# A gated pair of cached attentions on one core: the rows of the query weights dealt to the partitions in another order

## The chip, the cores and the metric

The kernel runs on one core of a Trainium2 chip. A core has a matrix engine (TensorE, PE in the profile), a vector engine (VectorE, DVE), a scalar engine (ScalarE, ACT), GpSimd (POOL) and SyncE (SP), which here does nothing but issue transfers. Sixteen DMA engines bring data from the chip's memory into the on-chip memory of 128 partitions. The metric is the device time of one execution in microseconds (us), as the median over several runs.

## The reference

There are two blocks, A and B, each a decode step of attention with its own weights and its own cache; one vector x per batch (2 batches, 512 numbers) goes into both, and a gate mixes the results.

```python
def block(x, k_cache, v_cache, wq, wo):          # x 2x1x512, caches 2x32x4096x128
    q = (x @ wq).reshape(2, 1, 32, 128).transpose(0, 2, 1, 3)
    scores = einsum("bhqd,bhkd->bhqk", q, k_cache) * 128 ** -0.5
    o = einsum("bhqk,bhkd->bhqd", softmax(scores), v_cache)
    return o.transpose(0, 2, 1, 3).reshape(2, 1, 4096) @ wo

g = sigmoid((x * gate_w).sum(-1, keepdims=True))
out = g * A(x) + (1 - g) * B(x)
```

All numbers are f32. Each wq is 512 x 4096 and each wo 4096 x 512, 8 MB apiece; each of the four caches is 128 MB.

## The kernel before

**Tiles and units.** All large data come in tiles of 128 partitions x 16384 numbers, 64 KB to a partition and 8 MB in all. There are three such buffers on chip: two called kt (for K, and at first for wq) and one called vt (for V). The work is cut into 32 units (2 blocks x 2 batches x 8 groups of four heads). For each unit one tile of K and one of V are loaded. VectorE multiplies K by the query in place (L257) and sums over the 128 numbers of a head (L262), which gives the scores; it takes their maximum (L264 to L268). ScalarE takes exponentials (L304, L307) and scales some slots of V (L313); TensorE multiplies them with V (L371), GpSimd handles the last slots of V (L336, L345). At the end both results are multiplied with wo (L424, L442) and written out.

**The order of the loads.** SP issues every large load, into one queue, in an order written out by hand (L122 to L235): wq of A and of B into the two kt buffers (L123); the first tile of K in two halves (L215, L216), once TensorE has finished A's projection; the second K tile and the first V tile (L212, L219), once B's projection is finished; then by turns the next K (L212), once VectorE has summed the K tile that lay there, and the next V (L228), once TensorE has finished with V. ScalarE's queue loads x (2 rows of 512) and the gate's row (L124, L125).

**The start, which the change touches.** wq has 512 rows. Partition p holds its rows 4p to 4p + 3, which are 64 KB in one piece ("block p" below). The projection contracts over the partition and over c, the row in the block, so x has to stand with its number 4p + c on partition p. The three rows (x of both batches and the gate's row) lie on three partitions of a buffer (`raw`, in qr0). TensorE turns them with four transposes, one for each c, which read every fourth number (L174); VectorE copies the result out of PSUM (`xg`, L158), scales x into `xs` (L160), multiplies x with the gate's row (L161) and sums (L163). A matmul with ones adds up over the partitions (L180), and VectorE makes g and 1 - g of it. The projection (L190) waits for wq and for `xs`; ScalarE brings its result to on-chip memory (L195), and further matmuls spread each query to the partitions of its head (L201).

**Semaphores** that the text names: x (x and the gate's row have landed), h (GpSimd's constants), e (VectorE's steps at the start and the end), y (TensorE's), k0 and k1 (the loads into the two kt buffers).

Of the kernel before, what the change touches and what calls it, by code (L numbers as in the profile page):

```python
# [13 lines left out]
B = 2  # L14
# [4 lines left out]
KC = D // P  # L19
# [17 lines left out]
UB = B * HG  # L37
CUT = UB - 2
PAD = 96
SCALE = DH ** -0.5  # L40
ACT3 = 3
DVE5 = 5
# [4 lines left out]
def tile_gated_decode(ctx: ExitStack, tc: tile.TileContext, ins: dict, out: bass.AP):  # L47
    nc = tc.nc
    lead = ctx.enter_context(tc.tile_pool(name="lead", bufs=1))
    lead.tile([P, PAD], F32, name="pad")  # L50
    big = ctx.enter_context(tc.tile_pool(name="big", bufs=1))
# [5 lines left out]
    def sb(name, shape):  # L57
        return small.tile(shape, F32, name=name)
# [4 lines left out]
    ident, ones = sb("ident", [P, P]), sb("ones", [P, P])  # L63
# [7 lines left out]
    vs, qr = sb("vs", [P, VC * DH]), [sb(f"qr{i}", [P, HG // 2, DH]) for i in range(2)]  # L71
    rl, ot, on = sb("rl", [P, HU]), sb("ot", [P, 2, B * H]), [sb(f"on{n}", [P, NJ, B]) for n in "AB"]
    xg, xw, zp, gate = sb("xg", [P, B + 1, KC]), sb("xw", [P, B, KC]), sb("zp", [P, B]), sb("gate", [P, 4, B])
    raw, xs = qr[0].rearrange("p g d -> p (g d)")[:B + 1], vs[:, :KC * QP].rearrange("p (c q) -> p c q", c=KC)
    rows, bs = qr[1][:H, :B], qr[0].rearrange("p g d -> p (g d)")
    res = qr[1].rearrange("p g d -> p (g d)")[:B]
# [5 lines left out]
    def sem(name):  # L82
        return tc.alloc_semaphore(name)

    sk, s_kb, s_v, s_x, s_out = [sem("k0"), sem("k1")], sem("kb"), sem("v"), sem("x"), sem("out")
    s_t = [sem(f"t{i}") for i in range(len(TAIL) + 2)]
    s_d, s_n, s_e = sem("d"), sem("n"), sem("e")
    s_a, s_c, s_p, s_o, s_y, s_g, s_h = (sem(x) for x in ("a", "c", "p", "o", "y", "g", "h"))
    ctx.enter_context(tc.tile_critical(sync_engine=mybir.EngineType.Pool))

    def wait(engine, *pairs):
        for s, v in pairs:
            engine.wait_ge(s, v)  # L93
# [3 lines left out]
    def inc(s, i):  # L97
        i.then_inc(s, 1)
        count[id(s)] = count.get(id(s), 0) + 1
        return count[id(s)]  # L100
# [16 lines left out]
    pe, dve, act, pool, sp = nc.tensor, nc.vector, nc.scalar, nc.gpsimd, nc.sync  # L117


    half = BIG // 2  # L120
    wq = {n: ins[n + "_wq"].rearrange("(p c) f -> p (c f)", c=KC) for n in "AB"}
    for i, n in enumerate("AB"):  # L122
        sp.dma_start(kbuf[i], wq[n]).then_inc(sk[i], 16)  # L123
    act.dma_start(raw[:B], ins["A_x"].rearrange("b s e -> (b s) e")).then_inc(s_x, 16)  # L124
# [14 lines left out]
    def e(i):  # L139
        return inc(s_e, i)  # L140
# [7 lines left out]
    for b in range(B):  # L148
# [5 lines left out]
    wait(dve, (s_h, READY), (s_e, head_at))  # L154
    const_at = e(dve.tensor_copy(heads.rearrange("p (a h) -> p a h", h=HP)[:, :, :HU],
                                 head[:, None, :].to_broadcast([P, VC, HU])))
    wait(dve, (s_y, 1))
    xg_at = e(dve.tensor_copy(xg, mix[:, 0, :KC * (B + 1)].rearrange("p (c r) -> p r c", c=KC)))  # L158
    wait(dve, (s_e, xg_at))
    xs_at = e(dve.tensor_scalar(xs[:, :, :B].rearrange("p c b -> p b c"), xg[:, :B], SCALE, None, op0=ALU.mult))  # L160
    xw_at = e(dve.tensor_tensor(xw, xg[:, :B], xg[:, B:].to_broadcast([P, B, KC]), op=ALU.mult))  # L161
# [7 lines left out]
    e(dve.tensor_scalar(gate[:, 3], gate[:, 2], -1.0, 1.0, op0=ALU.mult, op1=ALU.add))  # L169


    wait(pe, (s_x, 32), (s_h, 2))
    for c in range(KC):
        i = pe.transpose(mix[:, 0, c * (B + 1):(c + 1) * (B + 1)],  # L174
                         raw.rearrange("r (p c) -> r c p", c=KC)[:, c], ident[:B + 1, :B + 1])
        if c < 2:
            i.then_inc((s_p, s_o)[c], 1)
    i.then_inc(s_y, 1)
# [300 lines left out]
```

## Time and profile before

| what | before |
|---|---|
| median of 3 runs | 1324.2 us (1324.03 to 1324.35) |
| the profiled execution's own time | 1324.36 us |
| its span, first to last instruction | 1322.5 us |
| VectorE busy | 1136.7 us (86%) |
| TensorE busy | 446.2 us (34%) |
| GpSimd busy | 378.4 us (29%) |
| ScalarE busy | 174.2 us (13%) |
| bytes read | 570.43 MB, 431 GB/s over the span |

The profile is that of one execution. Its span lies 1.9 us under the execution's own time; the rest is outside the first and last instruction. A row of a timeline gives the start, the length in us, the engine, the line of the code, the operation and the tiles that it writes and reads; in brackets stands how long the engine sat idle before it and what ended that. A name with a q at its end (SPq, PEq) is an engine's sequencer, where issues of transfers stand. In a row of windows stand the window and its length, then for PE, the weight load of PE, DVE, ACT and POOL the busy us and the count of instructions, then the granted clock of TensorE, the mean busy share of the 16 DMA engines and the GB/s that they moved.

### The profile page before, as it was taken

The page shows a single profiled execution, that of the slowest core. Times are in us where ns is not written, and L with a number is a line of the kernel's source. Part 1 is how long each engine was busy: PE and PEld are TensorE (multiplying, and loading weights), DVE is VectorE, ACT ScalarE, POOL GpSimd, SP SyncE. Part 2 cuts the span into 40 slices and gives each one's busy share as a digit, 9 for nine tenths or more (in the row PEclk, how much of TensorE's full clock was granted, in tenths as well). Part 3 has the DMA queues.
Part 4 walks back from the last instruction along what each step waited for, and adds up shares of the span by engine and source line. Part 5 has one row for each costly group of instructions (what it writes and reads, how often), then busy time and mean ns, then how long its engine had stood idle before and what let it go on. Part 6 is the DMA issues. An engine that isn't in the chain of part 4 may idle for free.

```text
span 1322.5 us, 6956 instructions
## 1 busy us (share of the span) xinstructions
PE 446.2 (34%) x2344; PEld 176.9 (13%) x2344; DVE 1136.7 (86%) x249; ACT 174.2 (13%) x611; POOL 378.4 (29%) x202
## 2 busy tenths in 40 slices
PE   3303333223333231335323133332313333231376
PEld 1001110101111010111111011111101111110132
DVE  0399999989999999999999899999999999999960
ACT  0001110110111011011101111110111111111110
POOL 0003333212333321233332133333213333311350
PEclk9756666556666655666665566666556666655668
DMA  9999999999999999999999999999999999999998
GB/s 412 441 416 442 442 416 444 438 418 442 442 416 444 442 430 428 442 436 422 441 440 420 440 440 420 442 442 432 428 440 436 424 440 440 420 440 440 420 443 352
DMA packets 10962, 570.54 MB, mean 431 GB/s; under 512 B 1221, under 2 KB 1477, under 8 KB 1738
## 3 DMA queue, kind: packets, MB, share of 16 engines
q1 hardware_dynamic: 10948, 570.43, 99.6%
q8 instruction: 4, 0.07, 0.0%
q14 instruction: 4, 0.03, 0.0%
q10 hardware_dynamic: 6, 0.01, 0.0%
HBM read 570.43 MB, written 0.00 MB: 431 GB/s over the span
## 4 chain that ended last, share of the span: by engine, by line
DMA 51%; DVE 28%; issue 20%; PE 1%; DVEq 0%; SPq 0%; ACT 0%; POOLq 0%
DMA kt<-in_B_k_cache_dram 26%; DVE sc L262 23%; DMA kt<-in_A_k_cache_dram 21%; DVE kt L257 3%; DMA kt<-in_B_wo_dram 3%; DMA kt<-in_A_wq_dram 2%; DVE kt L274 1%; DVE sc L276 1%; PE mix L190 0%; PE q L190 0%; DVE rl L244 0%; DVEq L93 0%; PE q L442 0%; SPq L235 0%; DVEq L257 0%
## 5 line engine op out<-in xcount | busy, mean ns | idle before, releaser
L257 DVE TENSOR_TENSOR kt<-kt,q 128x16384 f32<-128x16384 f32 (+1 forms) x32 | 542.5, 16954 | 83.0 <-DMA kt<-in_B_k_cache_dram 47.6
L262 DVE TENSOR_REDUCE sc<-kt 128x128 f32<-128x16384 f32 (+1 forms) x32 | 542.5, 16953 | 1.9
L371 PE MATMUL vp<-vt,pr 128*32 128x512 f32 x1550 | 256.6, 773 | 700.5 <-DMA vt<-in_A_v_cache_dram 371.8
L336 POOL TENSOR_TENSOR vt<-vt,pp 128x2560 f32<-128x2560 f32 x31 | 138.4, 4465 | 891.6 <-DMA vt<-in_A_v_cache_dram 495.6
L345 POOL TENSOR_TENSOR vt<-vt 128x1536 f32<-128x1536 f32 (+2 forms) x93 | 219.5, 2360 | 7.4
L371 PEld LDWEIGHTS vp<-vt,pr 128*32 128x32 f32 x1550 | 82.5, 138 | 850.7 <-issue 845.1
L313 ACT ACTIVATE vt<-vt,pp 128x128 f32<-128x128 f32 x248 | 75.9, 388 | 592.7 <-DMA vt<-in_A_v_cache_dram 296.9
L371 PE MATMUL vp<-vt,heads 128*32 128x512 f32 x62 | 56.5, 1012 | 112.5 <-POOL vt L345 112.5
L304 ACT ACTIVATE pr<-sc,nm 32x100 f32<-32x100 f32 (+1 forms) x128 | 60.1, 470 | 112.4 <-DVE nm L268 110.9
L376 PE MATMUL ol<-strip,vs 128*128 128x4 f32 x256 | 58.8, 353 | 24.4 <-ACT vs L316 24.4
L316 ACT ACTIVATE vs<-vp 128x512 f32<-128x512 f32 x32 | 19.1, 597 | 360.9 <-PE vp L371 360.9
L376 PEld LDWEIGHTS ol<-strip,vs 128*128 128x128 f32 x256 | 56.1, 323 | 76.3 <-issue 74.7
L274 DVE TENSOR_TENSOR kt<-kt,q 128x8192 f32<-128x8192 f32 x1 | 8.7, 8686 | 39.9 <-DMA kt<-in_A_k_cache_dram 39.9
L304 ACT ACTIVATION_READ_ACCUMULATOR pr<-sc,nm 32x1 f32 x128 | 24.2, 189 | 0.0
L371 PEld LDWEIGHTS vp<-vt,heads 128*32 128x32 f32 x62 | 5.3, 133 | 140.6 <-POOL vt L345 140.6
L453 DVE COPY qr<-q 2x128 f32<-2x128 f32 x2 | 0.6, 282 | 22.1 <-PE q L442 22.1
L244 DVE RECIPROCAL rl<-ol 128x4 f32<-128x4 f32 x32 | 5.6, 176 | 14.7 <-PE ol L379 14.7
L379 PE MATMUL ol<-ltot,ones 128*128 128x4 f32 x64 | 18.0, 351 | 0.0
L190 PE MATMUL mix<-kt,vs 128*32 128x512 f32 x64 | 11.5, 887 | 17.4 <-DMA kt<-in_A_wq_dram 10.6
L379 PEld LDWEIGHTS ol<-ltot,ones 128*128 128x128 f32 x64 | 17.2, 329 | 0.0
L307 ACT ACTIVATE pp<-sc,nm 128x28 f32<-128x28 f32 (+1 forms) x32 | 10.2, 318 | 0.9
L264 DVE TENSOR_REDUCE rm<-sc 128x1 f32<-128x128 f32 x32 | 9.2, 286 | 1.1
(77 smaller groups left out, 139.1 us busy)
## 6 DMA issues: line engine op xcount, KB each, us to landing
kt<-in_A_k_cache_dram SPq DMA_DIRECT2D x2, 4096.0 KB, 25.7
kt<-in_B_wo_dram SPq DMA_DIRECT2D x1, 4096.0 KB, 32.5
kt<-in_B_wo_dram SPq DMA_DIRECT2D x3, 1024.0 KB, 36.6
kt<-in_B_wo_dram SPq DMA_DIRECT2D x1, 512.0 KB, 39.3
vt<-in_A_v_cache_dram SPq DMA_DIRECT2D x16, 24.7
kt<-in_B_k_cache_dram SPq DMA_DIRECT2D x16, 42.2
kt<-in_B_wo_dram SPq DMA_DIRECT2D x1, 256.0 KB, 39.5
kt<-in_B_wo_dram SPq DMA_DIRECT2D x2, 128.0 KB, 39.4
```

The costliest lines, as they stand in the source:

```text
L257: dve.tensor_tensor(k, k, q[:, None, :].to_broadcast([P, SLOTS - first, DH]), op=ALU.mult).then_inc(s_d, 1)
L262: dve.tensor_reduce(s[:, first:], k, axis=AX.X, op=ALU.add).then_inc(s_d, 1)
L274: m = e(dve.tensor_tensor(k1, k1, qall[:, None, A0:A0 + DH].to_broadcast([P, SLOTS // 2, DH]), op=ALU.mult))
L276: m = e(dve.tensor_reduce(sc[0][:, :SLOTS // 2], k1, axis=AX.X, op=ALU.add))
L304: x = act.activation(w, sc[u % 2][r, :f * VC].rearrange("p (c a) -> p c a", a=VC), AF.Exp, bias=nm[u % 2][r], accum_out=lsum[r, h:h + 1])
L313: x = act.activation(v[:, t], v[:, t], AF.Copy, scale=pp[u % 2][:, t:t + 1])
L316: act.activation(vs, vp, AF.Copy).then_inc(s_a, 1)
L336: pool.tensor_tensor(w[:, :m], w[:, :m], pp[j][:, :m, None].to_broadcast([P, m, DH]), op=ALU.mult).then_inc(s_g, 1)
L345: pool.tensor_tensor(x, x, y, op=ALU.add).then_inc(s_g, 1)
L371: x = pe.matmul(vp[s * QP:(s + 1) * QP], pr[:, c] if c < f else heads, v[:, c], start=c < STRIPS, stop=c > f - STRIPS)
L376: pe.matmul(ol[:, 0], vs[:, a * DH:(a + 1) * DH], strip[:, a * HP:a * HP + HU], start=a == 0, stop=a == VC - 1)
L379: pe.matmul(ol[:, 1], ones, ltot, start=True, stop=True).then_inc(s_o, 1)
```

## The change

Partition 8a + b (a from 0 to 15, b from 0 to 7) now takes block 16b + a of wq, for A and for B alike. In the pattern of the load, the memory's side has 16 groups (a) that lie one block of 64 KB apart, and in each group 8 blocks (b) that lie 16 blocks, 1 MB, apart. As the projection sums over all partitions, the order doesn't matter as long as x follows: a new copy on VectorE brings the three rows into that order, into `cols`, which lies in qr1, a buffer that is free then. With the copy the four numbers of a block also come apart, so that each transpose now reads 128 neighbouring numbers. VectorE's copy waits for x and the gate's row; TensorE's first transpose waits for the copy, where before it waited for x and the gate's row itself. The gate's sum over all partitions doesn't depend on the order. The loads of K, V and wo are as they were.

```diff
+LANES = 16
...
+    cols = qr[1].rearrange("p g d -> p (g d)")[:B + 1].rearrange("r (c p) -> r c p", c=KC)
...
-    wq = {n: ins[n + "_wq"].rearrange("(p c) f -> p (c f)", c=KC) for n in "AB"}
+    wq = {n: ins[n + "_wq"].rearrange("(b a c) f -> a b (c f)", c=KC, a=LANES) for n in "AB"}
     for i, n in enumerate("AB"):
         sp.dma_start(kbuf[i], wq[n]).then_inc(sk[i], 16)
...
+    wait(dve, (s_x, 32))
+    order_at = e(dve.tensor_copy(cols.rearrange("r c (a b) -> r c a b", a=LANES),
+                                 raw.rearrange("r (b a c) -> r c a b", c=KC, a=LANES)))
     wait(dve, (s_y, 1))
...
-    wait(pe, (s_x, 32), (s_h, 2))
+    wait(pe, (s_e, order_at), (s_h, 2))
     for c in range(KC):
         i = pe.transpose(mix[:, 0, c * (B + 1):(c + 1) * (B + 1)],
-                         raw.rearrange("r (p c) -> r c p", c=KC)[:, c], ident[:B + 1, :B + 1])
+                         cols[:, c], ident[:B + 1, :B + 1])
```

After the change the lines below the edits stand 2 to 5 higher in number.

## The prediction

> **What bounds the kernel now.** I read the page first: its line of DMA shares by slices, its queues, and the bytes.
>
> ```profile
> span 1322.5 us, 6956 instructions
> ...
> DMA  9999999999999999999999999999999999999998
> GB/s 412 441 416 442 442 416 444 438 418 442 442 416 444 442 430 428 442 436 422 441 440 420 440 440 420 442 442 432 428 440 436 424 440 440 420 440 440 420 443 352
> ...
> q1 hardware_dynamic: 10948, 570.43, 99.6%
> ...
> HBM read 570.43 MB, written 0.00 MB: 431 GB/s over the span
> ```
>
> Every slice of the DMA line but the last has a 9, and one queue, q1 (SP's), holds the 16 DMA engines for 99.6% of the span. So the time is the sum of what that queue moves. A tile of 128 x 16384 f32 is 8.389 MB, so q1's 570.43 MB are 68 such loads (two of wq, 64 of the caches, two of wo). Next the busy time of a long stretch in the middle, and the chain of waits in order of time (start, length, what):
>
> ```profile
> 100.00:1250.00 1150.00, 376.53 (x1868) 152.29 (x1868) 1057.86 (x210) 160.22 (x570) 357.14 (x180) 0.59 1.00 434
> ```
>
> ```profile
> 426.45 42.17 DMA kt<-in_A_k_cache_dram
> ...
> 503.73 42.16 DMA kt<-in_A_k_cache_dram
> ```
>
> In the middle the DMA share is 1.00 and the rate 434 GB/s; 8.389 MB at that rate are 19.33 us. The chain says the same: its loads of K begin 503.73 - 426.45 = 77.28 us apart, in which four loads (two K, two V) pass, so 19.32 us each. The 128 rows of a load, 64 KB each and one to a partition, fall on 16 engines, eight rows to each: 19.32 / 8 = 2.415 us a row, 27.1 GB/s an engine. That pace is even (42.17 and 42.16 in the two rows), with every engine busy. So bytes alone give 68 x 19.32 = 1313.8 us of the 1322.5, and only a change in the pace of a load, or in the gaps at the two ends, can move the end.
>
> The change touches the first two loads. Their issues (KB and the median us from issue to landing are the columns; with one load the median is its time), and when SP issued them:
>
> ```profile
> kt<-in_A_wq_dram SPq DMA_DIRECT2D x1, 22.1
> kt<-in_B_wq_dram SPq DMA_DIRECT2D x1, 41.0
> ```
>
> ```profile
> 0.89 0.40 SPq L123 DMA_DIRECT2D kt<-in_A_wq_dram  x1
> ...
> 1.35 0.42 SPq L123 DMA_DIRECT2D kt<-in_B_wq_dram  x1
> ```
>
> A's weights land at 0.89 + 22.1 = 23.0 us, which is 22.1 - 19.32 = 2.8 us more than a load at the pace of the middle: the start. B's land at 1.35 + 41.0 = 42.35, 19.36 behind A's: full pace already. Whatever the new order of addresses is good for, the most it can give back is that 2.8 and 0.04 us.
>
> **The change part by part.** Two edits: the pattern of the two wq loads, and a copy on VectorE in the way of x. First the copy. Of VectorE, the piece between its constants and the gate's sum (spread, deal and heads are constants; xg is x and the gate's row turned onto partitions; e, h, x, y are semaphores), before and then now:
>
> ```order
> L153 COPY deal<-ident 32x32 [waits e]
> L155 COPY heads<-head 128x4x4 [waits e,h]
> L158 COPY xg<-mix 128x12 [waits y]
> L160 TENSOR_SCALAR vs<-xg 128x2x4 [waits e]
> L161 TENSOR_TENSOR xw<-xg 128x8
> ```
>
> ```order
> L155 COPY deal<-ident 32x32 [waits e]
> L157 COPY heads<-head 128x4x4 [waits e,h]
> L160 COPY qr_92<-qr_91 3x512 [waits x]
> L163 COPY xg<-mix 128x12 [waits y]
> L165 TENSOR_SCALAR vs<-xg 128x2x4 [waits e]
> ```
>
> One copy of 3 x 512 has come in, and the wait on x has moved from TensorE's first transpose to it; TensorE now waits for the copy. What is queued behind that wait on VectorE is xg, which comes after the transposes anyway, and then nothing until the first product on K. The rows of the timeline that price it and that cover it:
>
> ```profile
> 2.23 0.70 DVE L149 COPY spread<-ident 128x128 f32<-128x128 f32 x2
> ...
> 10.49 0.64 PE L174 MATMUL mix<-ident,qr 3*128 3x3 f32 x4 [10.49 <-DMA qr<-in_gate_w_dram]
> 11.17 0.17 DVE L158 COPY xg<-mix 128x12 f32<-128x12 f32 x1 [8.09 <-PE mix L174]
> 11.38 0.17 DVE L160 TENSOR_SCALAR vs<-xg 128x8 f32<-128x8 f32 x1
> ...
> 23.04 5.49 PE L190 MATMUL mix<-kt,vs 128*32 128x512 f32 x32 [10.58 <-DMA kt<-in_A_wq_dram]
> ...
> 28.35 3.61 PE L190 MATMUL q<-kt,vs 128*32 128x512 f32 x32
> ...
> 32.02 0.33 SPq L215 DMA_DIRECT2D kt<-in_A_k_cache_dram  x1
> ...
> 42.39 6.05 PE L190 MATMUL mix<-kt,vs 128*32 128x512 f32 x32 [6.80 <-DMA kt<-in_B_wq_dram]
> ...
> 51.94 0.33 SPq L212 DMA_DIRECT2D kt<-in_A_k_cache_dram  x1
> ```
>
> A copy of 12 columns takes 0.17 us and one of 128 columns 0.35 (0.70 for two); 512 columns lie between 0.35 (length free) and 4 x 0.35 = 1.4. I take the line through the two rows: 0.17 + 500 x 0.18 / 116 = 0.95, and with a hand-over 1.1 us. It stands between x's landing at 10.49 and the scaled x, ready at 11.38 + 0.17 = 11.55. That is first read at 23.04, when A's weights are there: 11.5 us of cover. So the copy costs nothing; without the cover it would cost 1.1 us.
>
> Now the loads. Of SP, its first loads before and now (kt_62 and kt_63 are the two K buffers):
>
> ```order
> L123 DMA kt_62<-in_A_wq_dram 128x16384
> L123 DMA kt_63<-in_B_wq_dram 128x16384
> L215 DMA kt_62<-in_A_k_cache_dram 128x8192 [waits y]
> L216 DMA kt_62<-in_A_k_cache_dram 128x8192
> L212 DMA kt_63<-in_A_k_cache_dram 128x16384 [waits y]
> ```
>
> ```order
> L125 DMA kt_62<-in_A_wq_dram 128x1x16384
> L125 DMA kt_63<-in_B_wq_dram 128x1x16384
> L220 DMA kt_62<-in_A_k_cache_dram 128x8192 [waits y]
> L221 DMA kt_62<-in_A_k_cache_dram 128x8192
> L217 DMA kt_63<-in_A_k_cache_dram 128x16384 [waits y]
> ```
>
> No load has moved, and the bytes and the 64 KB rows are the same; the shape is not. Every big load of before has 128 rows on both sides. The two wq loads now have 128 rows on the side of the partitions and 16 groups of eight on the side of the memory. No transfer in the trace has unequal sides. My reading is that 16 groups on 16 engines are dealt one to each: engine a reads blocks a, 16 + a, 32 + a and so on, and writes partitions 8a to 8a + 7 one after the other.
>
> On the reading side that is harmless: 16 neighbouring blocks at a time. On the writing side the rows of before only say that its own dealing, whatever it is, lets each engine write 27.1 GB/s with none in another's way, since no load falls below it. A new dealing can keep that or lose it, it can't better it. If on-chip memory is entered by groups of partitions that are not eight neighbours, then engines that march in step through eight neighbours each meet in pairs at half of the entries, while the other half stand idle, and after four rows all change over together. Then every row takes two shares: 2 x 2.415 = 4.83 us, a load 38.64, and the two loads together cost 2 x 19.32 = 38.6 us more. The bounds are 0 (no two meet; then the wq rows themselves, at 19.36, are the price) and 38.6. The nearest row, the old wq load, has the old dealing, and the dealing is the one thing that is new, so I don't take its price; I take the upper end.
>
> [...]
>
> Does anything hide the 38.6? A's weights would land at 23.0 + 19.3 = 42.3, its projection takes 32.02 - 23.04 = 9.0, so the two halves of the first K go out at 51.3; B's weights hold the queue until 42.35 + 38.64 = 81.0, so it doesn't run dry. B's projection (51.94 - 42.39 = 9.55) lets SP issue the second K at 90.6, while the first K runs until 81.0 + 19.32 = 100.3: 9.7 us of cover, as before. Behind that the order and the waits of SP are unchanged, and all 66 remaining loads come 38.6 us later. Nothing has slack against a queue at 99.6%. x may land later too, behind rows of twice the length: by 21 at most (twice 10.49), and 21 + 1.1 + 1.1 = 23.2 is still ahead of 42.3.
>
> The sum: copy 0, wait 0, loads + 38.6. On the profiled execution's 1324.36 that is 1363.0, and that execution lies 0.16 over the median of 1324.2, so 1362.8.
>
> **The rivals.** *One engine of a pair goes first.* If an entry serves the first comer in full, the other waits four rows once, 4 x 2.415 = 9.7 us; from then on the two are at different entries, and the lag is carried through. That gives 1324.2 + 9.7 = 1333.9. Nothing in the trace speaks of how engines share an entry; that all rows keep one pace speaks for even sharing, hence the smaller chance.
>
> *Not slower: the dealing costs nothing.* Either the rows are dealt as before whatever the shape of the source, or an engine's 2.415 us a row is its own limit and not that of the entry, and where it writes is all one. For it: no row shows an entry as the limit. Point that decides: two engines on one entry must together move less than 2 x 27.1 GB/s. Then copy and loads come to 0, and the time is 1324.2.
>
> *Faster: the new order mends the start.* Sixteen neighbouring blocks at a time, instead of blocks far apart in the 8 MB, could be read quicker. The most is 2.84 us, 1321.4. Against it: B's load has the old order and full pace, and so have the loads of K and V, dealt alike. [...]
>
> **How the numbers follow.** Pairs in step 0.67; one first 0.13; nothing 0.17; start mended 0.03. The first gets the most because a dealing by 16 groups is what the pattern asks for, and only one arrangement of entries (eight neighbours each) would leave it unpunished. The likeliest gives 1362.8. For the range: below, the one-sided case, 1333.9, rounded out to 1333.5; above, sharing that also loses a start of 2.8 us in each load, 1362.8 + 5.6 = 1368.4, so 1368.5. Left out is 0.20. Within 0.2% (2.6 us, about what a measurement of this kernel can tell from no change): the third case and a third of the fourth, 0.18; faster by more 0.02; slower 0.80.
>
> **What would show it.** In the changed profile: wq landing at about 41 and 80 us after issue instead of 22.1 and 41.0; about half of 434 GB/s in the first two slices and the third; the first product on K (L274 before, L279 now) at 92 instead of 53; and from there the old pitch of 77.28. The copy should show as about 1 us on VectorE, with TensorE waiting for weights behind it. Landings of 22 and 41 would prove the forecast wrong, and so would a queue that runs dry between the wq loads and the first K, which would add to it.

## The result, and the profile after

The changed kernel takes 1366.46 us (median of 6 runs, 1366.30 to 1366.54) against 1324.2 before: a ratio of 1.0319 (95% interval 1.0308 to 1.0329), 42.3 us slower. The profiled execution's span is 1364.7 us, 42.2 more than before. On the page, the DMA lines by 40 slices of 34 us:

```profile
DMA  9999999999999999999999999999999999999998
GB/s 215 200 321 432 430 442 444 430 434 430 430 432 430 448 438 432 432 430 430 432 431 450 434 432 432 430 432 432 430 450 434 432 432 430 434 430 434 448 431 349
...
q1 hardware_dynamic: 10948, 570.43, 99.6%
```

The first line looks as it did: a 9 in every slice but the last, 99.6% for q1, the same packets and bytes. Only the second line tells: 215, 200 and 321 GB/s where 412, 441 and 416 stood, and from the fourth slice on the old rate. The windows put numbers to it (the last three columns are the granted clock, the busy share of the 16 DMA engines, and GB/s), the first within the two wq loads:

```profile
7.00:83.00 76.00, 14.12 (x78) 4.71 (x78) 1.69 (x9) 1.37 (x3) 0.00 (x0) 0.87 1.00 207
```

```profile
142.80:1292.80 1150.00, 375.91 (x1868) 153.72 (x1868) 1058.36 (x210) 160.19 (x570) 357.44 (x180) 0.59 1.00 434
```

Both have a share of 1.00; in the first the engines move 207 GB/s, in the second 434. So the busy share doesn't tell an engine at full pace from one at half of it. How they go through the rows can be seen in a stretch within B's load, 46 to 78 us in slices of 0.8 us, where each transfer is counted in the slice in which it begins:

```profile
GB/s 0 0 1311 0 0 0 0 0 983 328 0 0 0 0 246 1065 0 0 0 0 0 1229 82 0 0 0 0 1147 164 0 0 0 0 410 901 0 0 0 0 0
```

1311 GB/s over 0.8 us are 16 rows of 64 KB, as many as there are engines. They begin within one slice or two, and the next 16 begin about 5 us later: the engines march in step, and none runs ahead of the others. The issues of wq, and the rows of the timeline that answer to those of before:

```profile
kt<-in_A_wq_dram SPq DMA_DIRECT2D x1, 43.3
...
kt<-in_B_wq_dram SPq DMA_DIRECT2D x1, 83.1
```

```profile
0.89 0.69 SPq L125 DMA_DIRECT2D kt<-in_A_wq_dram  x1
...
1.64 0.57 SPq L125 DMA_DIRECT2D kt<-in_B_wq_dram  x1
...
13.48 0.61 DVE L160 COPY qr<-qr 3x512 f32<-3x512 f32 x1 [10.41 <-DMA qr<-in_gate_w_dram]
14.14 0.58 PE L179 MATMUL mix<-ident,qr 3*128 3x3 f32 x4 [14.14 <-DVE qr L160]
14.77 0.17 DVE L163 COPY xg<-mix 128x12 f32<-128x12 f32 x1 [0.68 <-PE mix L179]
...
44.27 5.88 PE L195 MATMUL mix<-kt,vs 128*32 128x512 f32 x32 [28.22 <-DMA kt<-in_A_wq_dram]
...
53.66 0.38 SPq L220 DMA_DIRECT2D kt<-in_A_k_cache_dram  x1
...
84.80 6.10 PE L195 MATMUL mix<-kt,vs 128*32 128x512 f32 x32 [27.58 <-DMA kt<-in_B_wq_dram]
...
94.40 0.33 SPq L217 DMA_DIRECT2D kt<-in_A_k_cache_dram  x1
...
95.72 8.69 DVE L279 TENSOR_TENSOR kt<-kt,q 128x8192 f32<-128x8192 f32 x1 [78.85 <-DMA kt<-in_A_k_cache_dram]
```

A's weights land at 44.2 instead of 23.0, B's at 1.64 + 83.1 = 84.74 instead of 42.35: 40.5 us behind A's, where a load took 19.4. That is 5.07 us for each of an engine's eight rows of 64 KB, 2.1 times 2.415. The first product on K starts 42.6 us later than before, where its row was

```profile
53.14 8.69 DVE L274 TENSOR_TENSOR kt<-kt,q 128x8192 f32<-128x8192 f32 x1 [39.88 <-DMA kt<-in_A_k_cache_dram]
```

and the rest follows at the old pitch; the chain of after has it:

```profile
468.78 42.16 DMA kt<-in_A_k_cache_dram
...
546.05 42.16 DMA kt<-in_A_k_cache_dram
```

546.05 - 468.78 = 77.27 us for four loads, as before. So the whole loss lies in the two wq loads, 21 us in each.

### The profile page after: what moved, and what is told of

Read it like the earlier page. It is cut to its first block, busy times and chain, and to the rows that moved or that the text cites. A ratio compares the mean times of both kernels' runs of the same rounds, so it can differ in the third digit from the quotient of the medians.

```text
span 1364.7 us, 6957 instructions
## 1 busy us (share of the span) xinstructions
PE 444.5 (33%) x2344; PEld 177.4 (13%) x2344; DVE 1137.3 (83%) x250; ACT 174.1 (13%) x611; POOL 378.8 (28%) x202
## 3 DMA queue, kind: packets, MB, share of 16 engines
q1 hardware_dynamic: 10948, 570.43, 99.6%
## 4 chain that ended last, share of the span: by engine, by line
DMA 52%; DVE 27%; issue 19%; PE 1%; DVEq 0%; SPq 0%; ACT 0%; POOLq 0%
DMA kt<-in_B_k_cache_dram 25%; DVE sc L267 22%; DMA kt<-in_A_k_cache_dram 22%; DVE kt L262 3%; DMA kt<-in_A_wq_dram 3%; DMA kt<-in_B_wo_dram 3%; DVE kt L279 1%; DVE sc L281 1%; PE mix L195 0%; PE q L195 0%; DVE rl L249 0%; DVEq L95 0%; PE q L447 0%; SPq L240 0%; DVEq L262 0%
## 5 line engine op out<-in xcount | busy, mean ns | idle before, releaser
L195 PE MATMUL mix<-kt,vs 128*32 128x512 f32 x64 | 12.0, 916 | 55.8 <-DMA kt<-in_A_wq_dram 28.2
L429 PE MATMUL q<-vt,onA 128*2 128x512 f32 x64 | 9.1, 728 | 4.8 <-DMA vt<-in_A_wo_dram 4.8
## 6 DMA issues: line engine op xcount, KB each, us to landing
kt<-in_B_k_cache_dram SPq DMA_DIRECT2D x16, 42.2
```

The costliest lines, as they stand in the source:

```text
L195: i = pe.matmul(r[h * QP:(h + 1) * QP], xs[:, c], cols[:, c, h, half_ * HG // 2:(half_ + 1) * HG // 2, :], start=c == 0, stop=c == KC - 1)
```

## The experiments

The trace says where the time went, not why. The theory is that of the prediction: 16 groups are dealt one to an engine, an engine then writes eight neighbouring partitions, and engines meet in pairs where they write. The dealing, and entries at which engines could meet, are assumptions of mine: no view names the engine of a row or shows an entry. Three rivals could lose the same 42 us in the same place: the path of x (copy and wait), the order of reading (neighbouring blocks at once), and the shape (a pattern of two levels is slow in itself).

**The copy alone.** The loads as before, the copy in x's own order:

```diff
-    wq = {n: ins[n + "_wq"].rearrange("(b a c) f -> a b (c f)", c=KC, a=LANES) for n in "AB"}
+    wq = {n: ins[n + "_wq"].rearrange("(p c) f -> p (c f)", c=KC) for n in "AB"}
...
-                                 raw.rearrange("r (b a c) -> r c a b", c=KC, a=LANES)))
+                                 raw.rearrange("r (a b c) -> r c a b", c=KC, a=LANES)))
```

> The copy on VectorE and its wait stay, the loads have their old pattern, and x keeps its old order. Theory (engines meet in pairs where they write): the copy is covered, 0.6 us of VectorE beside 9 us of slack before the weights land; 1324.2, within 0.5. Rival (the path of x is what costs): up to 1366.

Measured: 1324.1 us, ratio 1.0 (0.9991 to 1.0009). The copy takes 0.60 us at 10.53, and the path of x is out.

**Groups of four instead of eight.** Against the changed kernel, one number:

```diff
-LANES = 16
+LANES = 32
```

> The same change with 32 groups of four instead of 16 groups of eight: partition 4a + b takes block 32b + a, with x in that order. The pattern has two levels as in the changed kernel and neighbouring blocks are still read at the same time, but a group is four neighbouring partitions and no longer eight. Theory (meeting where they write): if 32 groups are dealt so that an engine again keeps one entry for itself, wq lands at 22.1 and 41.0 as before, and the time is 1324.2, within 1. Rival (reading): neighbouring blocks at once are slow to read; 1366, or between. Rival (shape): a pattern of two levels is slow in itself; 1366.

Measured: 1324.62 us, ratio 1.0003 (0.9994 to 1.0013). Its wq issues, and the window within the two loads:

```profile
kt<-in_A_wq_dram SPq DMA_DIRECT2D x1, 22.6
...
kt<-in_B_wq_dram SPq DMA_DIRECT2D x1, 41.2
```

```profile
7.00:39.00 32.00, 13.32 (x78) 4.54 (x78) 1.68 (x9) 1.37 (x3) 0.00 (x0) 1.00 0.98 426
```

Two levels in the pattern, neighbouring blocks read at once (16 of 32, if each engine takes its rows in order), the same copy, and the loads run at their old pace: the projections of A and B start at 23.56 and 42.86, 19.3 us apart. With that the shape is out as a cause, and so is the hope that such an order of reading mends the start: A lands 22.6 us after issue, B 41.2, against 22.1 and 41.0. Which two groups an engine gets stands in no view. Two neighbouring ones would be the eight partitions of the changed kernel again, and by the theory as slow; so the old pace fits the theory only if they are dealt otherwise. A slow run would not have refuted the theory. The next run is the stronger test: by the theory a piece of it reaches half of the entries, whichever engine writes which row.

**Halves of the partitions.** Against the kernel before, the blocks in their old order:

```diff
+    s_w = [sem("w0"), sem("w1")]
...
-        sp.dma_start(kbuf[i], wq[n]).then_inc(sk[i], 16)
+        sp.dma_start(kbuf[i][:P // 2], wq[n][:P // 2]).then_inc(s_w[i], 16)
+        sp.dma_start(kbuf[i][P // 2:], wq[n][P // 2:]).then_inc(sk[i], 16)
...
-        wait(pe, (sk[n], 16), (s_e, xs_at), (s_c, c0))
+        wait(pe, (s_w[n], 16), (sk[n], 16), (s_e, xs_at), (s_c, c0))
```

> The kernel before, with each wq load cut into two: partitions 0 to 63, then 64 to 127. Old order of the blocks, plain pattern, the same 64 KB rows, 16 engines with four rows each per piece. Theory (meeting): a piece reaches half of the entries, so two engines share one, at the 5.06 us a row of the changed kernel: (84.74 - 44.22) / 8. Each load 40.5, landing at about 42 and 83 us after issue, 1324.2 + 42.3 = 1366.5. Rivals (reading, shape): nothing has changed for them; 1324.2, within 1.

Measured: 1366.49 us, ratio 1.0319 (1.0303 to 1.0334). The window within the two loads, and the starts of the two projections:

```profile
7.00:83.00 76.00, 14.21 (x78) 5.04 (x78) 1.08 (x8) 1.37 (x3) 0.00 (x0) 0.87 0.99 204
```

```profile
44.22 5.92 PE L192 MATMUL mix<-kt,vs 128*32 128x512 f32 x32 [29.00 <-DMA kt<-in_A_wq_dram]
...
84.75 6.14 PE L192 MATMUL mix<-kt,vs 128*32 128x512 f32 x32 [27.54 <-issue]
```

No new order, no second level, no copy, and the loss of the change to a tenth of a microsecond in the median: B lands 40.5 us behind A. What this run shares with the change is, by the theory, that 16 engines write to too few places at a time. That a load comes in two pieces is not by itself the cause: the first K comes in two as well, cut by columns with all 128 partitions in each, and in the kernel before the slice in which it is loaded (33 to 66 us) ran at 441 GB/s.

**One of the two loads.**

```diff
-    wq = {n: ins[n + "_wq"].rearrange("(b a c) f -> a b (c f)", c=KC, a=LANES) for n in "AB"}
+    wq = {"A": ins["A_wq"].rearrange("(p c) f -> p (c f)", c=KC),
+          "B": ins["B_wq"].rearrange("(b a c) f -> a b (c f)", c=KC, a=LANES)}
```

> Only B's load has the new pattern, A's the old one. x is in the new order for both, so A's queries are computed with numbers of x that do not belong to the rows. Theory: the price is by the load: A lands at 22.1, B at 41.0 + 21.1 = 62 us after issue; 1324.2 + 21.1 = 1345.3. Rival (a price of the start, paid once by the first load): 1324; a price paid once by whichever load has the pattern: 1366.

Measured: 1345.2 us, ratio 1.0158 (1.0142 to 1.0173), 21.1 us over before. B lands 62.3 us after issue. The price is by the load and has nothing to do with the start.

**Eight groups of sixteen.** The changed kernel with `LANES = 8`.

> The same change with eight groups of sixteen: partition 16a + b takes block 8b + a, x in that order. [...] Rival (only the number of engines at work counts, entries don't): 16 x 2.415 = 38.6 a load, 1324.2 + 38.6 = 1362.8. [...]

Measured: 1463.36 us, ratio 1.105 (1.1018 to 1.1082), 100.6 us above the rival. Windows within A's load and later, with the first K under way, and the projections:

```profile
7.00:83.00 76.00, 1.17 (x6) 1.00 (x6) 1.68 (x9) 0.17 (x1) 0.00 (x0) 1.00 0.52 108
97.00:149.00 52.00, 0.34 (x1) 0.00 (x0) 0.00 (x0) 0.00 (x0) 0.00 (x0) 0.52 1.02 149
```

```profile
84.20 6.08 PE L195 MATMUL mix<-kt,vs 128*32 128x512 f32 x32 [68.11 <-DMA kt<-in_A_wq_dram]
...
181.67 5.14 PE L195 MATMUL mix<-kt,vs 128*32 128x512 f32 x32 [84.32 <-DMA kt<-in_B_wq_dram]
```

A share of 0.52 at 108 GB/s, read as half of the engines at work: 13.5 GB/s for each of eight, half of the 27.1 of before. The share stood at 1.00 with 16 groups and 0.98 with 32, so the number of groups seems to set how many engines work, as the theory's dealing has it; and the number of engines alone is not the bound, as eight at 27.1 would move 217 GB/s. Sixteen rows on each of eight engines, at the changed kernel's 5.07 us a row, are an estimated 81 us a load, and two such loads 1324.2 + 2 x (81 - 19.3) = 1447.6; the time lies 16 us above that. A's landing fits it (0.9 at issue + 2.8 for the start + 81 = 84.7; it came at 84.2), B's doesn't: it comes 97 us behind A and not 81. In the second window the first K is under way too (a share of 1.02, which fits the other eight engines moving it), and all together reach 149 GB/s.

**The same with the first K held back.** Against the run before:

```diff
+    wait(sp, (sk[1], 16))
     wait(sp, (s_y, 4))
     sp.dma_start(kbuf[0][:, :half], cache("k", 0)[:, :half]).then_inc(sk[0], 16)
```

> The kernel with eight groups of sixteen, but SP waits for B's weights before it issues the first K, so that the eight engines that have nothing of wq stay idle until then. It asks why B's weights landed 97 us behind A's there and not 81. If that came from the first K, which those eight engines were moving meanwhile: B lands 81 us behind A, at about 165; the first K starts 2 to 3 us later than it could, and the time is 1447.6 + 2.5 = 1450. If it came from B's load itself: B lands 97 behind A again, and the time is 1464 or more.

Measured: 1448.32 us, ratio 1.0939 (1.0907 to 1.0971). The two projections start at

```profile
83.61 5.18 PE L195 MATMUL mix<-kt,vs 128*32 128x512 f32 x32 [67.65 <-DMA kt<-in_A_wq_dram]
...
163.05 6.41 PE L195 MATMUL mix<-kt,vs 128*32 128x512 f32 x32 [67.19 <-DMA kt<-in_B_wq_dram]
```

79.4 us apart. So the excess came from the first K; a later issue made the kernel 15 us faster. How K's rows slow the load of wq so much stays open.

**Pieces of 16 partitions.** The kernel before with eight issues per load:

```diff
-        sp.dma_start(kbuf[i], wq[n]).then_inc(sk[i], 16)
+        for p in range(0, P, 16):
+            sp.dma_start(kbuf[i][p:p + 16], wq[n][p:p + 16]).then_inc(s_w[i] if p < P - 16 else sk[i], 16)
...
-        wait(pe, (sk[n], 16), (s_e, xs_at), (s_c, c0))
+        wait(pe, (s_w[n], 112), (sk[n], 16), (s_e, xs_at), (s_c, c0))
```

> The kernel before, with each wq load cut into eight of 16 neighbouring partitions: old order of the blocks, plain pattern, 64 KB rows, one row to each of 16 engines per piece. [...] Rival (an engine loses only to one fixed partner, so two shares are the worst): 5.06 a row, 1366.5. Rival (16 engines with one row each are at full pace): 1324.2.

Measured: 1434.65 us, ratio 1.0833 (1.0802 to 1.0865). The window within the loads, and the projections:

```profile
21.00:142.00 121.00, 13.00 (x72) 4.03 (x72) 0.00 (x0) 1.19 (x2) 0.00 (x0) 0.81 1.00 113
```

```profile
78.22 5.93 PE L192 MATMUL mix<-kt,vs 128*32 128x512 f32 x32 [63.64 <-DMA kt<-in_A_wq_dram]
...
152.50 6.34 PE L192 MATMUL mix<-kt,vs 128*32 128x512 f32 x32 [61.28 <-issue]
```

B lands 74.3 us behind A, 9.29 us a row, 3.85 times 2.415, and both rivals (5.06, 2.4) are out. It is less than four times 2.415; that is taken up below.

**Pieces of 32 partitions.** The same loop with 32 in place of 16; the question is which pace a row takes, the 5.07 us of the halves or the 9.29 of the pieces of 16.

> The kernel before, with each wq load cut into four of 32 neighbouring partitions, two rows to each of 16 engines per piece. [...]

Measured: 1366.06 us, ratio 1.0318 (1.0288 to 1.0348). The projections start at

```profile
44.05 5.08 PE L192 MATMUL mix<-kt,vs 128*32 128x512 f32 x32 [28.28 <-DMA kt<-in_A_wq_dram]
...
84.71 5.23 PE L192 MATMUL mix<-kt,vs 128*32 128x512 f32 x32 [28.52 <-issue]
```

40.7 us apart, 5.08 us a row. So pieces of 16, 32 and 64 neighbouring partitions take 9.29, 5.08 and 5.07 us a row, and one load of all 128 takes 2.415. Which partitions would share an entry, and that there are entries at all, these paces do not show. This settles the reading too: quarters and groups of four read much the same at a time, 16 of 32 neighbouring blocks if each engine takes its rows in order, and B's load takes 40.7 us in the one and 19.3 in the other.

## Why the prediction was right, point by point

**The bound.** That only the pace of a load, or a gap, could move the end held: the queue stayed at 99.6%, the pitch of the middle at 77.27, and the loss of the two loads (84.74 - 42.35 = 42.4 at B's landing) came through to the end in full (42.2 in span).

**The copy.** Taken at 0.95 us with 1.1 for the path; it took 0.61, and no row of it shows in the end. The copy alone measured 1.0. x came 3 us later than before (13.48 against 10.49; I had allowed for 21), and TensorE then waited 28.2 us more for A's weights.

**The loads.** The forecast was right in what the runs can show: a dealing by groups, as the busy share reads (0.52 with eight groups, 1.00 with 16), in step (16 rows begin together every 5 us), both loads (one of them alone cost 21.1), nothing hidden. That engines would meet in pairs at an entry was my assumption, and no run shows the term "every row takes two shares: 2 x 2.415 = 4.83 us" that rests on it; what the runs showed in its place is the pace of a row: 5.07 us, so a load of 40.5 us and not 38.64. They also speak for a loss where the rows are written and not in the shape, the copy or the reading: groups of four keep all three and lose nothing (1324.62 us), and halves and quarters lose the same without the change (1366.49 and 1366.06). Which partitions an engine writes is still inferred, as no view names the engine of a row. 16 rows x 0.24 = 3.8 us is what lies between the forecast's 1362.8 and the measured 1366.46 (3.7). The step behind it was to halve an engine's 27.1 GB/s to 13.6; an engine moved 12.9 (65.5 KB / 5.07 us).

**No gap behind the loads.** SP issued the first K at 53.66, while B's weights ran until 84.74, and the second at 94.40, ahead of the end of the first K, as worked out.

**The rivals.** One engine of a pair goes first: no, A's and B's loads lost 21 us each, where that case loses 9.7 once, and all 16 engines begin their rows together. The dealing costs nothing: no. Its point of decision was whether two engines on one entry move less than 2 x 27.1 GB/s. No view shows which two those would be, but all 16 were down to 12.9 GB/s each, so any two moved 2 x 12.9. The start mended: no, groups of four read neighbouring blocks too and took 1324.62, with A's weights no earlier.

## What to carry to other kernels

A load's pattern decides not only which bytes go where but also, as these runs read, how many engines carry them: with eight groups on the memory's side the busy share stood at 0.52, with 16 at 1.00. Keep the two sides of a big load alike at 128 rows, or, where the memory's side has to be regrouped, try groups of four partitions and not of eight or more: here that is the difference between 426 and 207 GB/s. And read GB/s beside the busy share: at half the pace the DMA line still showed nines through both loads, so the pace of each load (landing minus the landing before it) is the number to watch.

## What the runs showed of the hardware that I had not expected

The three paces of a row are not whole shares of one figure. At 2.415 us a row an engine moved 27.1 GB/s; at 5.07 us (the change, halves) it moved 12.9, which twice over is 25.9 (65.5 KB x 2 / 5.07 us); at 9.29 us (pieces of 16) it moved 7.1, which four times over is 28.2 (65.5 KB x 4 / 9.29 us). So a row of the second pace takes 5% longer than twice 2.415, and one of the third 4% less than four times. Why was not tried.

Issuing a load of two levels held SP for 0.69 and 0.57 us instead of 0.40 and 0.42. No run shows apart what that costs at the end.
